# Attention and a two-layer MLP on one core: two loads of q and k issued in front of two copies on GpSimd

## The chip, the core and the metric

The kernel runs on one core of a Trainium2 chip. The core has a matrix engine (TensorE, PE in the profile), a vector engine (VectorE, DVE), an activation engine (ScalarE, ACT), a general-purpose engine (GpSimd, POOL) and a queue engine (SyncE, SP) that here only issues transfers. Transfers between the chip's memory (HBM) and on-chip memory, and transposes done in flight, run on 16 DMA engines that all queues share. The metric is the device time of one execution in microseconds (us). Before the change it was 387.28 us, the median of three runs (386.26 to 387.37).

## The reference

Attention with 12 heads for 8 sequences of 448 tokens, then a two-layer MLP with a leaky ReLU over the 3584 tokens that come out:

```python
scores = (1 / sqrt(64)) * q @ k.T             # q, k, v: 8 x 12 x 448 x 64, float32
attn   = exp(scores - scores.max()) / sum      # softmax over the keys
x      = (attn @ v), heads side by side        # 3584 x 768
h      = x @ w_in                              # 768 x 2048
out    = maximum(0.01 * h, h) @ w_out          # 2048 x 768, float32 out
```

## The kernel before

**Units and chunks.** Attention is cut into 48 *units* u: one batch and one pair of heads each. A unit goes through these steps. Its q, k and v are loaded from HBM and cast to bf16 on the way (`load_soft`, L143, a DMA issued from GpSimd's queue for two units at a time; the names in the profile are fq, fk, fv). GpSimd copies q and k into an interleaved tile qkb (`cast`, L172) and v into a tile with a column of ones (L174). qkb is transposed into qkT: for units 0 to 14 on TensorE (`transposes`, L268, with a VectorE copy, L274), from unit 15 on by a DMA transpose from SyncE's queue (`dma_transposes`, which calls `turn`, L251). Each unit has four *chunks* of 112 keys. `scores` (L285) multiplies two heads of a chunk on TensorE, `expo` (L294) takes the exponential on ScalarE, and `rows` (L802, L808, L809) multiplies by v, divides by the sum and gives x. x is transposed into xT, mostly by DMA transposes of SyncE too (L251).

**The MLP.** The 3584 tokens are cut into seven blocks (`cuts`). For each, products with w_in (L366 and L662 in the first block, L483 in the others) give h, and products with w_out (L620, L555) give the output; most are done by a scheme with seven products in place of eight, for which VectorE forms sums and differences of weights and of x. MLP products are always on TensorE between the pieces of attention, so that ScalarE's exponentials run beside them.

**Order.** Every engine works its own queue in the order in which the program issues instructions; the program writes that order out by hand. After units 0 to 5, scores come in *bursts* of three chunks: burst g holds the chunks 3g to 3g+2, so burst 20 begins unit 15 and burst 21 ends it and begins unit 16. Between bursts, `place` interleaves MLP products and rows by a small model of the times. With each burst of the first block `place` calls `feed(g)`, which fills the queues of GpSimd and SyncE for units to come:

```python
def feed(g):
    t, r = divmod(g, 4)
    u = 3 * t
    if r < 3:
        if g >= 16: ahead = u + 6 + r
        for x, y in enumerate(("q", "cast")):
            cast(u + 3 + r, (x,))      # copy q, then k, of one unit
            fetch(1)
    ...
    pay()                              # copies of v that are due
    if r < 3:
        ahead = max(ahead, u + 5 + r)
        fetch()                        # loads up to unit `ahead`
```

`fetch` issues the next pair loads of q, k and v, as long as their first unit is not beyond `ahead` and the copies are close enough behind (unit u is loaded only once unit u-3 has been copied). So `feed(13)` copies q and k of unit 13, `feed(14)` those of unit 14. At g = 13 the lines give t = 3, r = 1, u = 9 and `ahead` = 15; at g = 14, `ahead` = 16, so the loads of q and k of units 16 and 17 are issued in `feed(14)`, behind unit 14's copies.

**Buffers.** Loads go to two buffers each for fq, fk and fv, so units 16/17 take those that units 12/13 had. qkb has three buffers, qkT four. Each load increments one of eight semaphores in turn. The w_out matrix arrives in four loads (L185) issued on GpSimd's queue just before.

Of the kernel before, what the change touches and what calls it, by code (L numbers as in the profile page):

```python
# [16 lines left out]
def kernel(  # L17
# [146 lines left out]
    def cast(u, parts=(0, 1, 2), by=nc.gpsimd.tensor_copy):  # L164
        if u >= NU:
            return
        for x in parts:
            f = raw[u].pop(x)
            if x < 2 and u not in qk_sb:
                qk_sb[u] = cast_pool.tile([SC, 2, NSC, 2, D], BF16, name="qkb")  # L170
            if x < 2:
                by(qk_sb[u][:, x].rearrange("p so h d -> p h so d"), f)  # L172
            else:
                by(v_sb[u % NV][:, :, :, :D], f)  # L174
# [6 lines left out]
    def load_w(n=1):  # L181
        for _ in range(n):
            if w_steps:
                o, i = w_steps.pop(0)
                nc.gpsimd.dma_start(out=o, in_=i)  # L185
# [67 lines left out]
    def dma_transposes(u):  # L253
        if NPE <= u < NU:
            turn(qkT[u % NQ][:, :QL], qk_sb[u].rearrange("p i so h d -> p (i so h d)"))
# [589 lines left out]
    ahead = 0  # L845

    def fetch(n=3):
        for x, y in enumerate(("q", "cast", "v")):
            u = to["load"][x]
            if n and u <= ahead and u - 3 < to[y]:  # L850
                load_soft(u, 2, (x,))
                to["load"][x] += 2
                n -= 1

    def pay():
        while owed_v and owed_v[0] < rows_done + NV:
            cast(owed_v[0], (2,))
            to["v"] = owed_v.pop(0) + 1
        fetch()

    def feed(g):
        nonlocal ahead
# [3 lines that stand above are left out]
            if g >= 16:  # L866
                ahead = u + 6 + r
            for x, y in enumerate(("q", "cast")):
                cast(u + 3 + r, (x,))
                to[y] = u + 4 + r  # L870
                fetch(1)
            owed_v.append(u + 3 + r)
        pay()
        if r < 3:
            ahead = max(ahead, u + 5 + r)
            fetch()
            load_w({9: 1, 10: 3}.get(g, 0))
        if r > 0:
            dma_transposes(u + 2 + r)
            to["turn"] = max(to["turn"], u + 3 + r)  # L880
# [4 lines left out]
    def place(i, want, soon=0, full=True, calm=True, first=False, lazy=0, keen=NU, cap=NU):  # L885
# [3 lines left out]
        while True:  # L889
# [21 lines left out]
            if want > done and state < 2 and turned(last) and not blocked and len(slots) == 3 and all(  # L911
                x <= now + 0.05 + 0.2 * j for j, x in enumerate(at)
            ):
                state = 2
                order = list(slots)
                start = chunk
                burst(lazy)
                if first:
                    feed(start // 3)
                done += 1  # L920
                for x, t in enumerate(order[:chunk - start]):
                    model["act"] = max(model["act"], now + 0.45 + 0.2 * x) + 0.8
                    free[id(t)] = model["act"] + (0.3, 0.15 + 0.5 * (lazy > 1), 0.15 + 0.5 * lazy)[x]
                    if (start + x) % NSC == NSC - 1:
                        ready[(start + x) // NSC] = model["act"] + 0.1
                model["now"] = now + 0.78
                continue
# [115 lines left out]
```

## Time and profile before

| | us |
|---|---|
| median of the runs (three) | 387.28 |
| lowest, highest | 386.26, 387.37 |
| the profiled execution, whole | 386.85 |
| its span on the core | 385.1 |
| in its span: TensorE busy | 374.7 |
| ScalarE busy | 264.3 |
| VectorE busy | 232.8 |
| GpSimd busy | 141.9 |

The span reaches from the first to the last instruction of the profiled execution, whose own time is 1.75 us longer. The granted TensorE clock is 1.0 throughout. In the rows that follow, a timeline line gives the start in us, the length in us, the engine, the line of the kernel, the operation, output and inputs, the count, and in brackets the idle time ahead of it and what ended that. SPq and POOLq are the queues of DMA issues. A line of windows gives the stretch, its length, the busy time of PE, PE's weight loads, DVE, ACT and POOL, each with a count of instructions, then the granted clock, the DMA engines' mean share and the GB/s they moved. The share of the DMA engines can be over 1, since transfers of several queues overlap. A line of DMA issues ends with the size and the us from issue to landing.

### The profile page before, as it was taken

The numbers are of one execution on the slowest core, as the hardware profiler recorded it, in microseconds if no ns is written. First come the engines' busy times: TensorE is split into PE (matmuls) and PEld (weight loads), VectorE is DVE, ScalarE is ACT, GpSimd is POOL, SyncE is SP. The second block draws the span as 40 slices with busy tenths as digits, with TensorE's granted clock in tenths as the row PEclk, the third lists the DMA queues.
The fourth block names the chain that finished last, engine by engine and source line by source line (L and its number), as shares of the span: only waits on it lengthen the run. The fifth ranks groups of instructions, "written<-read, shape, count | busy, mean of one in ns | idle before, by whom it ended". The sixth has DMA issues, their size and how long they took to land.

```text
span 385.1 us, 10021 instructions
## 1 busy us (share of the span) xinstructions
PE 374.7 (97%) x4095; PEld 259.4 (67%) x4095; DVE 232.8 (60%) x488; ACT 264.3 (69%) x391; POOL 141.9 (37%) x223
## 2 busy tenths in 40 slices
PE   7999999979999999999999999999999999999995
PEld 3665558745588655886558865678656895668753
DVE  3662946835867646657469574576745665474753
ACT  6997886745767877687765877767776687717700
POOL 6988750765455443620436304353042100000000
PEclk9999999999999999999999999999999999999999
DMA  8999999799979958991499913899229600330022
GB/s 165 183 195 203 183 189 203 90 138 205 165 126 129 140 91 161 199 131 26 74 183 171 146 26 56 179 184 156 27 48 182 140 15 3 107 81 26 3 82 83
DMA packets 93278, 47.09 MB, mean 122 GB/s; under 512 B 51888, under 2 KB 89904, under 8 KB 93232
## 3 DMA queue, kind: packets, MB, share of 16 engines
q0 software_dynamic: 37536, 22.24, 45.7%
q1 hardware_dynamic: 55056, 23.66, 32.1%
q8 instruction: 32, 0.52, 0.6%
q10 hardware_dynamic: 640, 0.56, 0.5%
q14 instruction: 14, 0.11, 0.1%
HBM read 45.61 MB, written 11.01 MB: 147 GB/s over the span
## 4 chain that ended last, share of the span: by engine, by line
PE 76%; DMA 16%; POOL 5%; issue 2%; ACT 0%; DVE 0%; POOLq 0%; ACTq 0%
PE g L555 31%; PE g L483 14%; PE sc L483 14%; PE sc L802 8%; PE sc L285 7%; DMA fk<-in_k_dram 5%; DMA fq<-in_q_dram 4%; DMA w_mix<-in_v_dram 3%; POOL qkb L172 2%; DMA qkT<-qkb 2%; DMA w_in_mix<-in_v_dram 1%; POOL v L174 1%; PE g L620 1%; DMA hmix<-in_q_dram 1%; POOL fk L143 1%
## 5 line engine op out<-in xcount | busy, mean ns | idle before, releaser
L294 ACT ACTIVATE e<-sc 112x896 bf16<-112x896 f32 x192 | 162.7, 920 | 49.2 <-PE sc L285 49.2
L555 PEld LDWEIGHTS <-h 128*128 128x128 bf16 x632 | 57.2, 98 | 44.2 <-issue 12.4
L555 PE MATMUL g<-w_out_sb,h 128*128 128x384 bf16 x416 | 81.0, 326 | 0.0
L472 ACT ACTIVATE h<-c 128x512 bf16<-128x512 f32 (+1 forms) x72 | 43.5, 611 | 25.5 <-DVE c L498 17.2
L483 PEld LDWEIGHTS <-w_in_sb 128*128 128x128 bf16 x576 | 54.3, 98 | 6.0
L285 PE MATMUL sc<-qkT 64*128 64x448 bf16 x384 | 50.2, 353 | 4.7 <-DMA qkT<-qkb 3.0
L172 POOL COPY qkb<-fq 112x512 bf16<-112x512 bf16 x38 | 26.2, 689 | 73.5 <-DMA fq<-in_q_dram 41.4
L174 POOL COPY v<-fv 112x512 bf16<-112x512 bf16 x38 | 25.0, 667 | 69.9 <-PE sc L802 69.8
L802 PEld LDWEIGHTS <-e 112*128 112x128 bf16 x1344 | 46.2, 97 | 4.5 <-ACT e L294 0.2
L802 PE MATMUL sc<-v,e 112*128 112x65 bf16 x1344 | 47.7, 193 | 0.0
L483 PEld LDWEIGHTS <-w_in_mix 128*128 128x128 bf16 x432 | 41.2, 98 | 4.1
L560 DVE COPY o<-g 128x384 f32<-128x384 f32 x49 | 27.2, 554 | 22.3 <-PE g L555 22.2
L555 PE MATMUL g<-w_mix,h 128*128 128x384 bf16 (+1 forms) x208 | 38.3, 323 | 0.0
L285 PEld LDWEIGHTS <-qkT 64*128 64x128 bf16 x384 | 15.7, 94 | 32.2 <-issue 19.5
L563 DVE TENSOR_TENSOR o<-o,g 128x384 f32<-128x384 f32 x39 | 21.6, 553 | 18.0 <-PE g L555 15.9
L809 DVE TENSOR_TENSOR x<-sc,rec 112x512 bf16<-112x512 f32 x42 | 29.0, 692 | 1.5
L808 DVE RECIPROCAL rec<-sc 112x8 f32<-112x8 f32 x42 | 8.7, 207 | 34.8 <-PE sc L802 31.4
L172 POOL COPY qkb<-fk 112x512 bf16<-112x512 bf16 x38 | 24.5, 645 | 13.4 <-DMA fk<-in_k_dram 13.3
L483 PE MATMUL g<-xT,w_in_sb 128*128 128x256 bf16 (+1 forms) x216 | 28.5, 268 | 0.0
L483 PE MATMUL sc<-xT,w_in_sb 128*128 128x256 bf16 (+1 forms) x216 | 28.5, 268 | 0.0
L555 PE MATMUL g<-w_mix,hmix 128*128 128x384 bf16 x104 | 20.1, 326 | 0.0
L483 PE MATMUL g<-x_mix,w_in_mix 128*128 128x256 bf16 (+1 forms) x144 | 19.0, 268 | 0.0
(106 smaller groups left out, 475.4 us busy)
## 6 DMA issues: line engine op xcount, KB each, us to landing
fq<-in_q_dram POOLq DMA_DIRECT2D x19, 224.0 KB, 6.5
fk<-in_k_dram POOLq DMA_DIRECT2D x19, 224.0 KB, 7.5
fv<-in_v_dram POOLq DMA_DIRECT2D x19, 224.0 KB, 5.8
w_in_sb<-in_moe_w_in_dram POOLq DMA_DIRECT2D x4, 768.0 KB, 11.6
w_out_sb<-in_moe_w_out_dram POOLq DMA_DIRECT2D x4, 768.0 KB, 18.4
out_dram<-o SPq DMA_DIRECT2D x7, 336.0 KB, 4.5
out_dram<-o SPq DMA_DIRECT2D x8, 288.0 KB, 3.7
out_dram<-o SPq DMA_DIRECT2D x7, 240.0 KB, 3.8
```

The lines of the kernel that those rows point to most:

```text
L172: by(qk_sb[u][:, x].rearrange("p so h d -> p h so d"), f)
L174: by(v_sb[u % NV][:, :, :, :D], f)
L285: nc.tensor.matmul(ps[:, j, :S], t[j * D:(j + 1) * D, S + c * SC:S + c * SC + P], t[j * D:(j + 1) * D, :S], start=True, stop=True,)
L294: nc.scalar.activation(e[:, :, c, :], sc_t.pop((u, c))[:SC, :, :S], AX.Exp, scale=scale)
L472: nc.scalar.activation(hs[:, m:m + 2, cols], x.rearrange("p (m t) -> p m t", m=2), AX.Prelu, alpha=0.01)
L483: nc.tensor.matmul(ps[:, j * nh:(j + 1) * nh], w[:, kk, ts(j, P)], x[:, kk], start=(first and j == 0 and kk == 0), stop=(kk == KH - 1), sk ...
L555: nc.tensor.matmul(ps[:, cols], x[:, m], w[:, m], start=(first and m == 0), stop=(m == MH - 1), skip_group_check=True,)
L560: by(o[:, at], ps[:, :NW])
L563: nc.vector.tensor_add(o[:, at], o[:, at], ps[:, :NW])
L802: nc.tensor.matmul(ps[:, j, qc, :D + 1], e[:, at:at + P], vt[:, j, c, :D + 1], start=(c == 0), stop=(c == NSC - 1),)
L808: nc.vector.reciprocal(rec, ps[:SC, :, :, D:D + 1])
L809: nc.vector.tensor_mul(x_t[u].rearrange("p q j d -> p j q d"), ps[:SC, :, :, :D], rec.to_broadcast([SC, 2, NSC, D]))
```

## The change

One line of `feed` is changed:

```diff
         pay()
         if r < 3:
-            ahead = max(ahead, u + 5 + r)
+            ahead = max(ahead, u + (6 if g >= 13 else 5) + r)
             fetch()
             load_w({9: 1, 10: 3}.get(g, 0))
```

For g = 13 `ahead` becomes 16 instead of 15, so `feed(13)` issues the loads of q and k of units 16 and 17 at its end. For g = 14 it becomes 17 instead of 16, which allows no load that was not allowed before, and from g = 16 on the earlier line in `feed` gives the same value as before. GpSimd's queue is the only one whose order is changed:

```diff
 L172 copy qkb<-fq   (unit 13)
 L172 copy qkb<-fk   (unit 13)
-L172 copy qkb<-fq   (unit 14)
-L172 copy qkb<-fk   (unit 14)
 L143 load fq        (units 16, 17)
 L143 load fk        (units 16, 17)
+L172 copy qkb<-fq   (unit 14)
+L172 copy qkb<-fk   (unit 14)
 L174 copy v<-fv     (unit 13)
 L143 load fv        (units 16, 17)
```

All instructions, their sizes and their number are the same, and so are the orders of TensorE, VectorE, ScalarE and SyncE.

## The prediction

> **What bounds the kernel now.** I read the busy shares first, then TensorE's list of waits, the chain of waits that ended last, and the timelines of the queues that this chain names.
>
> ```profile
> span 385.1 us, 10021 instructions
> PE 374.7 (97%) x4095; PEld 259.4 (67%) x4095; DVE 232.8 (60%) x488; ACT 264.3 (69%) x391; POOL 141.9 (37%) x223
> ...
> PE   7999999979999999999999999999999999999995
> ...
> PE sc L285 <- DMA qkT<-qkb: 3.0, 2, 2.6
> ```
>
> TensorE (PE) is busy for 374.7 of 385.1 us, so only a gap on PE can be won. In the forty slices it is below 9 tenths in the first, the last and the ninth (77 to 87 us). The last row heads PE's list of waits (total us, times, longest) and is its only one for a DMA: 3.0 us in two waits of the scores (L285) for transposed q and k (qkT), which is the ninth slice's gap. PE's timeline places the two waits:
>
> ```profile
> 83.64 0.74 PE L285 MATMUL sc<-qkT 64*128 64x448 bf16 x6 [2.60 <-DMA qkT<-qkb]
> ...
> 86.37 0.36 PE L285 MATMUL sc<-qkT 64*128 64x448 bf16 x2
> 87.13 0.55 PE L285 MATMUL sc<-qkT 64*128 64x448 bf16 x4 [0.40 <-DMA qkT<-qkb]
> ```
>
> Bursts of three chunks and four chunks to a unit make the six products at 83.64 the first of unit 15 (burst 20, chunks 60 to 62). Burst 21 begins with unit 15's last chunk at 86.37 and goes on to unit 16 at 87.13. Without waits they would have started at 81.04 (83.64 - 2.60) and 84.13 (87.13 - 0.40 - 2.60). From unit 15 on the transposes are DMAs of SyncE (SP), so the next question is what made those late. Two pieces of the chain of waits (start, us, what), then the timelines of SP and GpSimd (POOL) answer it:
>
> ```profile
> 32.12 15.31 DMA fq<-in_q_dram
> ...
> 80.11 6.97 DMA qkT<-qkb
> ```
>
> ```profile
> 76.33 1.22 SPq L251 DMA_TRANSPOSE qkT<-qkb  x1
> ```
>
> ```profile
> 52.88 0.62 POOL L172 COPY qkb<-fk 112x512 bf16<-112x512 bf16 x1
> 68.02 0.81 POOL L172 COPY qkb<-fq 112x512 bf16<-112x512 bf16 x1 [14.52 <-DMA fq<-in_q_dram]
> 69.00 0.71 POOL L172 COPY qkb<-fk 112x512 bf16<-112x512 bf16 x1 [0.17 <-DMA fk<-in_k_dram]
> 69.66 0.70 POOL L143 DMA_DIRECT2D fq<-in_q_dram  x1
> 70.35 0.70 POOL L143 DMA_DIRECT2D fk<-in_k_dram  x1
> 71.05 0.62 POOL L174 COPY v<-fv 112x512 bf16<-112x512 bf16 x1
> 72.71 0.71 POOL L143 DMA_DIRECT2D fv<-in_v_dram  x1 [1.04 <-issue]
> ...
> 74.98 0.70 POOL L143 DMA_DIRECT2D fq<-in_q_dram  x1 [0.31 <-POOL qkb L172]
> 75.68 0.62 POOL L172 COPY qkb<-fk 112x512 bf16<-112x512 bf16 x1
> ...
> 79.46 0.62 POOL L172 COPY qkb<-fk 112x512 bf16<-112x512 bf16 x1
> ```
>
> POOL ends unit 13's copies at 53.50 (52.88 + 0.62), sits idle for 14.52 us until unit 14's loads land, and is then a queue without a gap it could close by itself: copies of 14, loads of 16/17, v, copies of 15 (ending at 76.30, when SP issues transpose 15 at 76.33), loads of 18/19, copies of 16 (ending at 80.08; transpose 16 at 80.11). So the two waits of PE hang on POOL's work after 68.02 and on how long each transpose takes in flight.
>
> **The change, part by part.** Two load issues, q and k of units 16/17, leave their place behind unit 14's copies (69.66 and 70.35) for the place behind unit 13's copies (53.50). Nothing is added or removed; the loads cross only unit 14's two copies in POOL's queue, and no other queue changes its order.
>
> (1) *POOL's time after 68.02.* What followed the two issues started at 71.05 and can now start at 69.66: 1.39 us earlier. The copies of 15 and 16 wait for no transfer there, so transpose 15 is issued at 74.94 (76.33 - 1.39) and 16 at 78.72 (80.11 - 1.39). The row at 72.71 shows 1.04 us of idle where a load behind a copy elsewhere waits 0.31 (the row at 74.98); if this extra 0.73 went away too, the shift would be 2.12. I take 1.39, as no row says what the extra belongs to.
>
> (2) *The new place.* The 1.40 us of issuing (2 x 0.70) lies in the 14.52 us in which POOL waited. The buffers are those of units 12/13, free once unit 13's copies end, so the q load waits some 0.3 us; the k load also waits for the first w_out piece, which had the same semaphore:
>
> ```profile
> L185 POOL DMA_DIRECT2D w_out_sb<-in_moe_w_out_dram x1: 752/752/752, 39.8 to 39.8; - x1
> ...
> DMA to landing us min/median/max: 14.4/14.4/14.4
> ```
>
> It landed at 54.2 (39.8 + 14.4), before the k load's turn (53.50 + 0.30 + 0.70 = 54.50). Cost nothing, covered by 12.8 us (68.02 - 55.2). Without that cover each microsecond would delay unit 14's copies by as much, and PE's own transposes of 14, at 71.76, would be next:
>
> ```profile
> 71.76 0.56 PE L268 MATMUL sc<-c,qkb 112*128 112x112 bf16 x8
> ```
>
> (3) *The DMA engines.* Here are the windows from 66 to 78 us (the last two columns are the DMA share and GB/s), then the landings of the loads issued at 49.67, 50.37 and 51.07:
>
> ```profile
> 66.00:68.00 2.00, 1.97 (x22) 1.33 (x21) 1.23 (x3) 1.95 (x4) 0.00 (x0) 1.00 1.22 164
> 68.00:70.00 2.00, 2.00 (x31) 2.00 (x29) 1.97 (x3) 1.53 (x3) 1.81 (x3) 1.00 0.20 27
> 70.00:72.00 2.00, 2.00 (x48) 2.00 (x45) 1.90 (x4) 1.53 (x4) 1.68 (x3) 1.00 0.46 50
> 72.00:74.00 2.00, 2.00 (x20) 0.95 (x18) 1.54 (x3) 1.08 (x2) 1.29 (x3) 1.00 1.25 160
> 74.00:76.00 2.00, 2.00 (x15) 1.05 (x15) 1.30 (x4) 1.90 (x3) 1.69 (x4) 1.00 1.12 130
> 76.00:78.00 2.00, 2.00 (x25) 1.23 (x23) 0.85 (x3) 1.91 (x3) 1.62 (x3) 1.00 0.88 94
> ...
> fq<-in_q_dram POOLq DMA_DIRECT2D x1, 224.0 KB, 18.2
> fk<-in_k_dram POOLq DMA_DIRECT2D x1, 224.0 KB, 18.6
> fv<-in_v_dram POOLq DMA_DIRECT2D x1, 224.0 KB, 19.0
> ```
>
> They landed at 67.9, 69.0 and 70.1, in the order of issue and 1.1 us apart: POOL's transfers pass through in order, so two more behind them delay none of them. Behind them the engines almost emptied (shares 0.20 and 0.46); there the moved transfers fit and should land at 71.2 and 72.3 at the same spacing. Now they are issued at 69.66 and 70.35 and stand at the head of what follows, as the landings of q16 and k16 and then of v16 (issued at 72.71), k18 and the two transposes show:
>
> ```profile
> fq<-in_q_dram POOLq DMA_DIRECT2D x1, 224.0 KB, 4.0
> fk<-in_k_dram POOLq DMA_DIRECT2D x1, 224.0 KB, 4.9
> ...
> fv<-in_v_dram POOLq DMA_DIRECT2D x1, 224.0 KB, 4.7
> ...
> fk<-in_k_dram POOLq DMA_DIRECT2D x1, 224.0 KB, 7.1
> qkT<-qkb SPq DMA_TRANSPOSE x1, 7.3
> qkT<-qkb SPq DMA_TRANSPOSE x1, 7.0
> qkT<-qkb SPq DMA_TRANSPOSE x1, 3.0
> ```
>
> q16 landed at 73.7, k16 at 75.3, v16 at 77.4, k18 at 83.7 and transpose 15 at 83.6 (76.33 + 7.3): each load entered before the one ahead of it had landed. With q16 and k16 gone, v16 is issued at 71.32 (72.71 - 1.39) into an empty queue and takes between 4.0 us (q16, alone) and 4.7, landing at 75.3 to 76.0, which is 1.4 to 2.1 us earlier; what queues behind should keep its spacing to v16. So transpose 15's flight shrinks by 0 to 0.7 us beyond the shift. The last row, transpose 17 issued at 84.8, bounds the flight from below: 3.0 us.
>
> The arbitration between the two kinds of transfer is the open size. The Trainium skill, "DMA: Bandwidth & Descriptors", section "Queues, rings and completion order", says that a DMA engine takes turns between the queues that have work, packet by packet. By that rule a transpose gets its turns however long the other queue is, so shortening the backlog without emptying it would leave the 7.3 us as they are and the gain would be the bare shift. The rows fit it in part: flights of 7.3 and 7.0 us beside loads, 3.0 us where the backlog was nearly through.
>
> (4) *The sum.* Lower bound, shift alone: transpose 15 lands at 82.24 (wait 1.20 instead of 2.60), transpose 16 at 85.69 (78.72 + 6.97) against a need at 84.13 + 1.20 = 85.33; unit 16's scores start about 1.4 us earlier. Upper bound: transpose 15 in time for 81.04 (flight 6.1 or less) and 16 for 84.13 (5.4 or less): all 3.0. Both lie within the flights seen, 3.0 to 7.3. I take 1.9: the shift of 1.39 and 0.5 of the possible 0.7, since v16 would meet a queue as empty as q16's. After 90 us PE waits for no DMA, and loads, copies and transposes of later units hang on the same queues and move with it, so PE keeps the gain. The profiled execution took 386.85 us (385.1 and 1.75 around the span): 384.95 after. The runs' median is 387.28, 0.43 above it, so the forecast for the median is 387.28 - 1.9 = 385.4.
>
> **The rivals.** *A. The bare shift.* The flights keep 7.3 and 6.97: 387.28 - 1.4 = 385.9. The turn-taking rule of the Trainium skill, cited above, would bring this about. For it: a share of 0.88 or more in the windows from 72 to 78, where v16, q18 and k18 stay beside transpose 15. Against it: the 3.0 us flight.
>
> *B. The gap at 72.71 is tied to the clock and not to the copy ahead of it.* Then POOL's v16 load, and all behind it, stays where it is; the shift is lost, and only the emptier DMA queue is left: v16 lands at 76.7 instead of 77.4, worth at most 0.7 us: 386.6, not to be told from no change. For it: 1.04 us "issue" for which the profile names no releaser. Against it: nothing that landed then is known.
>
> *C. Slower: POOL is held at one of the two moved issues.* Here a load is held until transfers ahead of it have landed, because too much is outstanding. POOL runs in order, so unit 14's copies are held with it. Held until v of 14/15 lands at 70.1, POOL starts unit 14's q copy at 70.8 (0.70 for the issue), ends both at about 72.2, against 71.05 for the same point now: transpose 15 is 1.15 us later, and PE's own transposes of 14 wait 0.4 us at 71.76. PE then loses about 1.2: 388.5, and more with a longer hold. It decides once the second issue ends after 69.4 (68.02 + 1.39). Against it: near 44 us four w_out pieces of 768 KB and the loads of units 10/11 (the first of them, in the chain above, from 32.12 to 47.4) were outstanding, and the last three w_out issues show no hold:
>
> ```profile
> 42.19 2.23 POOL L185 DMA_DIRECT2D w_out_sb<-in_moe_w_out_dram x3
> ```
>
> At 54.5 it would be three w_out pieces and five loads of 224 KB: 3424 KB (3 x 768 + 5 x 224) against 3744 (4 x 768 + 3 x 224) then.
>
> *D. Everything.* Both waits go: 387.28 - 3.0 = 384.3. It needs transpose 15 in 6.1 us.
>
> **How the numbers follow.** About 0.3% (1.16 us) is what a measurement of this kernel can tell from no change. Chances: forecast (gain 1.6 to 2.6) 0.32, A 0.18, D 0.14, B or another loss of the shift 0.21, C or another loss 0.15. Faster by over 0.3% are the forecast, A and D, 0.64, less 0.02 for runs of A that fall short of 1.16: 0.62. Within 0.3%: B and those, 0.23. Slower: 0.15. The likeliest case's own range is 384.3 to 385.9, from D to A. For eight in ten it goes to 384.0 (D with the 0.3 of scatter) and up to 387.5 (B whole, with scatter), which leaves out C.
>
> **What would show it.** Right: two load issues on POOL between 53.5 and 55.3; unit 14's copies still at 68.0; the v copy behind them at about 69.7; DMA shares from 68 to 72 near those before 68, and emptier from 72 to 74; transpose 15 issued near 74.9; PE's wait for qkT under 1.6 us in all, with no new wait elsewhere. A shows as flights of 7 us, B as a v16 load still at 72.7, C as copies of unit 14 after 68.5. I am wrong altogether if unit 14's loads land later than 68, or if PE's gain near 87 us is given back to another wait before the end.

## The result and the profile after

The changed kernel took 385.94 us (median of 20 executions, 383.84 to 386.96) against 386.90 us for the kernel before in the same comparison (20 executions, 386.13 to 390.18). The ratio is 0.9959 with a 95% interval of 0.9942 to 0.9976, so it is faster by 0.9 to 2.2 us, 1.6 us at the centre. (The means, 387.25 and 385.67 us, lie 1.58 us apart, the medians 0.96.) Two more comparisons gave 0.9987 (0.9962 to 1.0011) and 0.9957 (0.9936 to 0.9978). The profiled execution took 386.51 us, 384.7 of them in the span; that is 0.34 us less than the profiled execution of before, where the prediction had 1.9.

The page of the changed kernel (busy time, then PE's row of the forty slices), and below it PE's list of waits:

```profile
span 384.7 us, 10021 instructions
PE 375.0 (97%) x4095; PEld 259.5 (67%) x4095; DVE 232.7 (60%) x488; ACT 263.9 (69%) x391; POOL 140.8 (37%) x223
...
PE   7999999989999999999999999999999999999995
```

```profile
PE sc L285 <- DMA qkT<-qkb: 2.0, 2, 1.1
PE g L216 <- DVE c L211: 1.2, 1, 1.2
PE sc L285 <- ACT e L294: 0.8, 3, 0.4
PE g L268 <- ACT qkb L239: 0.6, 1, 0.6
```

The ninth slice rose from 7 to 8, and the two waits for qkT fell from 3.0 to 2.0 us. The last row is a wait in the first microseconds that the profiled execution of before did not have; with it and what else differs in the start, PE reached burst 18 at 73.54 instead of 72.90. PE's timeline has both waits at the same two places as before:

```profile
73.54 0.74 PE L285 MATMUL sc<-qkT 64*128 64x448 bf16 x6
...
82.82 0.74 PE L285 MATMUL sc<-qkT 64*128 64x448 bf16 x6 [1.15 <-DMA qkT<-qkb]
...
86.82 0.55 PE L285 MATMUL sc<-qkT 64*128 64x448 bf16 x4 [0.90 <-DMA qkT<-qkb]
```

GpSimd's timeline shows the moved loads and what followed from them:

```profile
54.06 0.71 POOL L143 DMA_DIRECT2D fq<-in_q_dram  x1
55.11 0.70 POOL L143 DMA_DIRECT2D fk<-in_k_dram  x1 [0.33 <-issue]
68.37 0.69 POOL L172 COPY qkb<-fq 112x512 bf16<-112x512 bf16 x1 [12.56 <-DMA fq<-in_q_dram]
69.47 0.61 POOL L172 COPY qkb<-fk 112x512 bf16<-112x512 bf16 x1 [0.42 <-DMA fk<-in_k_dram]
70.03 0.94 POOL L174 COPY v<-fv 112x512 bf16<-112x512 bf16 x1
72.01 0.71 POOL L143 DMA_DIRECT2D fv<-in_v_dram  x1 [1.04 <-issue]
...
74.89 0.75 POOL L172 COPY qkb<-fk 112x512 bf16<-112x512 bf16 x1
```

Both loads are issued while GpSimd would have waited anyway. The copy of v follows unit 14's first copy by 1.66 us (70.03 - 68.37); before it was 3.03 (71.05 - 68.02), so 1.37 us are gained there. The copy of v then takes 0.94 us where it took 0.62, and the gap of 1.04 us ahead of the next load is still there. At the load of v 1.05 us are left of the shift (72.01 - 68.37 = 3.64, before 72.71 - 68.02 = 4.69). In SyncE's timeline 1.01 us are left at unit 15's transpose (75.67 - 68.37 = 7.30, before 76.33 - 68.02 = 8.31):

```profile
75.67 1.23 SPq L251 DMA_TRANSPOSE qkT<-qkb  x1
```

The windows of the changed kernel from 68 to 76 us (the last two columns are the DMA share and GB/s):

```profile
68.00:70.00 2.00, 2.00 (x25) 1.63 (x22) 1.94 (x3) 1.53 (x3) 1.21 (x2) 1.00 1.46 197
70.00:72.00 2.00, 2.00 (x48) 2.00 (x46) 1.97 (x5) 2.00 (x4) 0.97 (x2) 1.00 0.89 121
72.00:74.00 2.00, 2.00 (x25) 1.30 (x23) 1.63 (x3) 0.61 (x2) 1.87 (x3) 1.00 0.25 27
74.00:76.00 2.00, 2.00 (x15) 1.09 (x12) 1.11 (x4) 2.00 (x3) 1.51 (x3) 1.00 0.88 107
```

The hole in the transfers has moved: at 68 to 70 us the share is 1.46 instead of 0.20, and the engines are nearly idle from 72 to 74, where they had a share of 1.25. The landing rows of v of 16/17, q of 18/19 and the transposes of units 15 and 16 show who profits:

```profile
fv<-in_v_dram POOLq DMA_DIRECT2D x1, 224.0 KB, 3.6
...
fq<-in_q_dram POOLq DMA_DIRECT2D x1, 224.0 KB, 4.1
...
qkT<-qkb SPq DMA_TRANSPOSE x1, 7.1
...
qkT<-qkb SPq DMA_TRANSPOSE x1, 7.3
```

The loads that come next land sooner (3.6 instead of 4.7 us, 4.1 instead of 5.0). The transposes, for which TensorE waits, fly as long as before (7.3 and 7.0).

### The profile page after: what moved, and what is told of

Same layout as the page of the kernel before. It is cut to its first block, busy times and chain, and to the rows that moved or that the text cites. A ratio compares the mean times of both kernels' runs of the same rounds, so it can differ in the third digit from the quotient of the medians.

```text
span 384.7 us, 10021 instructions
## 1 busy us (share of the span) xinstructions
PE 375.0 (97%) x4095; PEld 259.5 (67%) x4095; DVE 232.7 (60%) x488; ACT 263.9 (69%) x391; POOL 140.8 (37%) x223
## 4 chain that ended last, share of the span: by engine, by line
PE 91%; ACT 3%; DMA 3%; DVE 1%; issue 1%; POOL 1%; DVEq 0%; ACTq 0%; POOLq 0%
PE g L555 31%; PE g L483 14%; PE sc L483 14%; PE sc L285 11%; PE sc L802 10%; PE g L366 4%; ACT e L294 3%; PE g L662 2%; DMA qkT<-qkb 2%; PE g L620 2%; DMA hmix<-in_k_dram 1%; PE g L268 1%; PE g L304 1%; PE sc L366 1%; PE g L331 0%
```

## The experiments

Two theories stood against each other. By *shift*, TensorE gains what GpSimd's queue gains, and no more. By *relief*, it gains because two transfers are gone from the head of the DMA queue. All ratios are to the kernel before, run on the same chip.

**The shift taken back, the early loads kept** (e1_pad):

```diff
             owed_v.append(u + 3 + r)
+            if g == 14:
+                for f in pad:                  # unit 14's raw q and k
+                    nc.gpsimd.tensor_copy(f, f)
         pay()
```

> The changed kernel with two idle copies on GpSimd (unit 14's q and k raw tiles copied onto themselves) right where the moved loads used to be, about 1.4 us of GpSimd time. The early loads stay early. Theory 'shift' (the gain is GpSimd's 1.39 us alone): the gain is gone, ratio to before 0.999 to 1.001, TensorE's two waits for qkT back at about 3.0 us, transpose flights 7 us. Rival 'relief' (the gain comes from two transfers less at the head of the DMA queue): at least half of the gain stays, ratio 0.996 to 0.998, flights of the transposes of units 15 and 16 shorter than 6.5 us.

Ratio 1.0015 (0.9998 to 1.0031): the gain is gone. GpSimd's timeline shows the two idle copies and unit 15's k copy:

```profile
69.75 0.94 POOL L878 COPY fq<-fq 112x512 bf16<-112x512 bf16 x1
70.63 0.94 POOL L878 COPY fk<-fk 112x512 bf16<-112x512 bf16 x1
...
76.13 0.62 POOL L175 COPY qkb<-fk 112x512 bf16<-112x512 bf16 x1
```

They took 1.8 us, somewhat more than the 1.4 planned. By the times, relief is out, as it asked for 0.996 to 0.998. The one profile does not show where the gain went. Its flights were 6.6 and 6.1 us, the second shorter than relief asked for, and its two waits for qkT came to 2.0 us, as in the changed kernel, with TensorE at burst 18 (73.52, changed kernel 73.54) and at burst 22 (90.92 and 90.99) at almost the same times. The 1.6 us by which its span is longer (386.3 against 384.7) come later, most of them in two waits for VectorE that neither the profile of before nor that of the changed kernel has:

```profile
PE sc L288 <- DMA qkT<-qkb: 2.0, 2, 1.7
...
PE g L486 <- DVE x_mix L433: 0.8, 1, 0.8
PE g L558 <- DVE o L566: 0.6, 1, 0.6
```

A wait like the last one also stands in a profile without the idle copies (0.8 us in e10 below), so whether the copies cause these waits stays open. That the gain hangs on the shift rests here on the twelve times and not on this profile.

**Half of the change** (e3_q_only): the load of q in front of unit 14's copies, the load of k between them.

```diff
-            fetch()
+            fetch(1 if g == 13 else 3)
```

> Half of the change: only the load of q of units 16/17 goes in front of unit 14's copies; that of k is issued between unit 14's two copies. 'Shift': 0.70 us of GpSimd time is gained, TensorE's waits for qkT about 2.3 us against 3.0 before, ratio 0.998 (half of the change). 'Relief' would also give about half. A threshold (gain only once both are moved) would give 1.000.

Ratio 0.9987 (0.9965 to 1.0010), where 0.998 was expected; the interval holds no change as well. The waits came to 0.9 us, with TensorE late (burst 18 at 74.25). It tells little.

**The shift the other way.** The same idle copies in the kernel before, two (e6_before_pad) and one (e9_before_pad_half):

```diff
             owed_v.append(u + 3 + r)
+            if g == 14:
+                for f in pad:                  # one copy: pad[:1]
+                    nc.gpsimd.tensor_copy(f, f)
         pay()
```

> The kernel before with two idle copies on GpSimd (about 1.4 us) behind unit 14's copies: the shift the other way. 'Shift': TensorE's waits for qkT grow by about 1.4 us to 4.4 us, ratio 1.003 to 1.004. If the lateness of GpSimd there does not set the time (a threshold, or slack between it and TensorE): ratio 0.999 to 1.001.

> The kernel before with one idle copy on GpSimd behind unit 14's copies, about 0.9 us, half of the pad that cost 4.1 us (ratio 1.0107). 'Clock' (a wait of TensorE of 4 to 5 us lets the granted clock drop to 0.5 for some 3 to 4 us, and shorter ones do so now and then): the time grows by more than 0.9 us, ratio 1.004 to 1.007, with single executions 1.5 to 2 us apart; where the profile shows a wait over 4 us in one piece, the clock is below 1.0 in the windows behind it. 'One for one': ratio 1.002 to 1.003 and a clock of 1.0 throughout.

Two copies (0.93 us each, 1.8 together and not the 1.4 planned) gave a ratio of 1.0107 (1.0066 to 1.0149), 4.1 us. PE's timeline and the windows behind the wait (the third column from the end is the granted clock) show where they went:

```profile
87.98 1.11 PE L288 MATMUL sc<-qkT 64*128 64x448 bf16 x6 [5.07 <-DMA qkT<-qkb]
```

```profile
88.00:89.00 1.00, 1.00 (x6) 0.20 (x6) 0.00 (x0) 0.55 (x1) 1.00 (x2) 0.61 1.35 241
89.00:90.00 1.00, 1.00 (x6) 0.48 (x5) 0.00 (x0) 1.00 (x2) 1.00 (x3) 0.50 0.35 75
90.00:91.00 1.00, 1.00 (x5) 0.50 (x4) 0.00 (x0) 0.98 (x2) 1.00 (x3) 0.50 0.60 116
91.00:92.00 1.00, 1.00 (x6) 0.53 (x5) 0.00 (x0) 0.00 (x0) 1.00 (x2) 0.68 0.92 117
```

The wait is 2.1 us longer than the 3.0 of before, and behind it TensorE's clock is down for four windows, which costs another 1.7 us of work (0.39 + 0.50 + 0.50 + 0.32). Unit 15's transpose also flew 8.8 us here, where it flew 7.3 before. The six executions tell the clock's share apart: five had a granted clock of 0.990 to 0.996 and took 390.95 to 392.40 us, and the one that kept 1.000 took 388.81, which is 1.95 us above the median of before (386.86) and close to the 1.8 us of the copies.

One copy gave 1.0020 (0.9997 to 1.0042), one for one and short of what the clock theory expected, in an interval that holds no change as well. Its profiled execution had waits of 1.13 and 0.50 us and a clock of 1.00; its two longest executions, 389.29 and 390.11 us, had 0.994 and 0.996, the other ten 0.998 or more.

**Fewer loads beside the transposes.** In the changed kernel, the loads of units 18/19 are issued later. A flag holds them in `fetch`: q and k alone until unit 16's copies (e2_qk18_late), all three until unit 16's (e4_all18_late) or unit 17's copies (e7_all18_later, g == 18).

```diff
-            if n and u <= ahead and u - 3 < to[y]:
+            if n and u <= ahead and u - 3 < to[y] and not (held and x < 2):   # all three: not held
...
+        if g == 16:
+            held = True
...
+        if g == 17:                            # behind unit 16's copies
+            held = False
+            fetch()
         pay()
```

> The changed kernel with the loads of q and k of units 18 and 19 moved behind unit 16's copies. If the 7 us flights come from loads in flight beside the transposes: unit 15's transpose is issued 0.7 us or more earlier than in the changed kernel and flies under 5 us, both waits of TensorE for qkT fall to 0.3 us or less, ratio to before 0.991 to 0.993. If the flights come from something else (the transposes themselves, the transpose of x between them): flights stay at 6.5 to 7.5 us, and the gain over the changed kernel is GpSimd's shift alone, about 1.0 us at unit 15 and 1.5 to 2 us at unit 16; ratio 0.992 to 0.994, so the flights tell the two apart. A third outcome: unit 18's copies become late and TensorE waits at burst 24.

> As e2_qk18_late, and the load of v of units 18/19 goes behind unit 16's copies as well, so that unit 15's transpose meets no load that is issued after it until unit 16's copies end. If loads beside the transposes set the flights: unit 15's transpose flies 3 to 4.5 us, unit 16's still meets the three loads; both waits gone, ratio 0.991 to 0.993. If not: flights of 6.5 us or more.

> The changed kernel with all loads of units 18/19 behind unit 17's copies, so that neither unit 15's nor unit 16's transpose has a load issued beside it. If loads beside a transpose set its flight: both fly 3 to 4.5 us (against 7.1 and 7.3 in the changed kernel, 3.5 and 8.8 where only unit 16's met the loads). If the order of the transposes or their own traffic sets it: unit 16's still takes 6 us or more. The time is open: the copies of units 18 to 21 come several us later and may make TensorE wait at burst 24 or later.

The landing rows of the transposes of units 15 and 16 in e7, where unit 15's has no load issued beside it and unit 16's one only in its last microsecond:

```profile
qkT<-qkb SPq DMA_TRANSPOSE x1, 3.3
...
qkT<-qkb SPq DMA_TRANSPOSE x1, 2.9
```

So the loads set the flights: about 3 us without them, about 7 beside them. In e4 the flights were 5.2 and 6.9 us, no wait for qkT was left, and the ratio was 0.9956 (0.9941 to 0.9972). e7 itself took 389.74 us in its one execution, since the held loads, and with them the copies of units 18 to 20, became late and TensorE waited 2.9 us at burst 26:

```profile
107.31 0.36 PE L285 MATMUL sc<-qkT 64*128 64x448 bf16 x2 [2.92 <-DMA qkT<-qkb]
```

In e2 unit 15's transpose flew 3.5 us and unit 16's, issued amid three loads, 8.8. The profiled execution was at 384.73 us with one wait of 0.3 us, yet the times spread from 384.0 to 391.2 us and the ratio, without the longest, was 1.0018 (0.9989 to 1.0048). Because of that spread the kernel was profiled twice more.

> The kernel with q and k loads of 18/19 behind unit 16's copies, once more, because its times fell in two groups (384.0 to 385.2 and 387.9 to 389.6) and the profile came from the faster one. If the slower group comes from the wait for unit 16's transpose (8.8 us beside three loads): an execution near 389 us shows a wait for qkT of over 2 us or a clock below 1.0 behind one. If it comes from elsewhere: no such wait, and the time is lost at another place.

> The same kernel a third time, for a look at the other group of times: same expectations as for the second.

They took 388.25 and 386.90 us. PE's timeline and the landing of unit 16's transpose in the first of them:

```profile
87.95 0.55 PE L285 MATMUL sc<-qkT 64*128 64x448 bf16 x4 [3.13 <-DMA qkT<-qkb]
```

```profile
qkT<-qkb SPq DMA_TRANSPOSE x1, 10.8
```

In the other the flight was 10.2 us and the wait 1.9. One transpose beside the same three loads thus landed after 8.8, 10.2 or 10.8 us, and the time went with it. The clock was 1.00 in both. In the first comparison the four slowest executions, 389.11 to 391.18 us, had a granted clock of 0.994 to 0.996, the other eight, up to 389.00 us, 0.998 or more. So the slowest lost clock as well; behind which wait, no profile shows.

**The two candidates again** (e5_change_again, e12_change_third: the change; e8_e4_again: all loads of 18/19 behind unit 16's copies):

> The changed kernel itself once more, so that it stands beside the others on one chip. Ratio to before 0.994 to 0.998 as in its first runs. TensorE's waits for qkT between 0.5 and 2 us, depending on how late TensorE reaches burst 20 in the profiled execution; flights of the transposes of units 15 and 16 again 6.5 to 7.5 us.

> The kernel with all loads of units 18/19 behind unit 16's copies, once more. If it removes the wait for good: ratio to before 0.993 to 0.997 and below that of the changed kernel by 0.1 to 0.4%, no wait for qkT in the profile. If its first result was the luck of a chip: not below the changed kernel.

> The changed kernel a third time, since its first two comparisons gave ratios of 0.9959 and 0.9987 whose intervals overlap between 0.9962 and 0.9976. If GpSimd's net shift of about 1.0 us at the load of v is what TensorE gains: ratio 0.996 to 0.998, waits of TensorE for qkT of 1 to 2 us. The full gain of the forecast (1.9 us) would be 0.995.

The change gave 0.9987 and 0.9957, the other kernel 0.9958 (0.9926 to 0.9989), at a median of 385.11 us against 386.25 for the change on the same chip. Its profile has no wait for qkT, with a flight of 3.1 us for unit 15's transpose, although three loads were issued behind it from 1.6 us on, as in e4, where the same transpose took 5.2:

```profile
PE g L216 <- DVE c L211: 1.2, 1, 1.2
PE g L268 <- ACT qkb L239: 0.9, 1, 0.9
PE sc L285 <- ACT e L294: 0.8, 3, 0.4
PE sc L285 <- DVE qkT L274: 0.2, 1, 0.2
```

It was steady at 0.9956 and 0.9958, but the change's three ratios overlap with these, so that it is the better kernel is likely and not shown.

## Why the prediction was right, and which of its terms was not

**What bounds the kernel.** Right. TensorE's only wait for a DMA stands at bursts 20 and 21, and the time moves with GpSimd's queue: with the shift taken back the gain was gone (1.0015), and the opposite shift cost time (1.0107). Half of each, 0.9987 and 1.0020, points the same way within the noise. TensorE also kept what it had won, as predicted: burst 22 began 0.31 us earlier (90.99 against 91.30), and the span was 0.4 us shorter.

**Part (1), 1.39 us of shift.** Its size held at the place named (1.37 us, up to the copy of v) and 0.32 us were lost one step further: that copy, moved forward, ran beside VectorE's differences of two weight tiles and took 0.94 us instead of 0.62. VectorE's timelines of the changed kernel, then of the kernel before:

```profile
70.42 1.43 DVE L383 TENSOR_TENSOR w_mix<-w_out_sb,w_mix 128x768 bf16<-128x768 bf16 x2
```

```profile
69.16 1.84 DVE L383 TENSOR_TENSOR w_mix<-w_out_sb,w_mix 128x768 bf16<-128x768 bf16 x2
71.03 0.21 DVE L808 RECIPROCAL rec<-sc 112x8 f32<-112x8 f32 x1
```

Before, the copy started at 71.05, as the last of these ended; now it starts at 70.03, among them. The Trainium skill ("SBUF — State Buffer", section "Who interferes with whom") says that a VectorE instruction with two inputs in SBUF contends with a GpSimd instruction that reads SBUF; the rows agree, with 0.94 us beside such an instruction and 0.62 behind it. The prediction priced the moved work by its old length and did not look at what it would then stand beside. In e3 the loss fell on the other side: GpSimd's copies at 69.88 and 70.44 took 0.62 us each, and the two differences of L383 beside them 2.37 us together, against 1.43 in the row at 70.42. No run moved VectorE's work, so that it is the cause is read off the timelines.

**Part (2), the new place costs nothing.** Right: GpSimd still waited 12.56 us for unit 14's loads, and the k load waited only 0.33 us. Rival C, a hold at the moved issues, did not occur.

**Part (3), the flights.** This is the term that was mis-sized: the 0.5 us by which a shorter queue was to shorten the flights measured nothing beyond the scatter (7.1 and 7.3 us against 7.3 and 7.0; in the repeats 7.4 and 7.3, 6.9 and 6.5; in e1, with the same loads moved, 6.6 and 6.1). The load of v did land 1.8 us earlier (75.6 against 77.4), as forecast, but the transpose behind it did not keep its distance to it. The prediction took the length of the queue ahead of a transpose for what delays it. The runs show that it is the loads beside it. In e2 and its two repeats, in e7 and in e8 a transpose flew 2.9 to 3.5 us with at most one earlier load still in flight and the next issued 0.8 us or more behind it. It flew 6.5 to 7.4 us in the changed kernel, where the loads of units 18/19 are in flight or issued beside it, and 8.8 to 10.8 us where a load of q was issued just ahead of it and one of k just behind. The rule is not sharp, as the 5.2 us in e4 and the 8.8 us in e6 show. The unchanged flights are rival A. The turn-taking rule of the Trainium skill ("DMA: Bandwidth & Descriptors", section "Queues, rings and completion order"), which the prediction weighed and set aside, agrees with the 7.1 and 7.3 us; the 8.8 to 10.8 us it does not give by itself.

**Rival B.** The gap of 1.04 us was tied to its place in the queue and not to the clock: it ended at 72.71 before and at 72.01 now, and it had the same length in every run. What it is stays open.

**The signs.** Two of those that the prediction named went against it. TensorE's two waits came to 2.0 us and not under 1.6. And unit 14's loads landed after 68, with the first copy at 68.37, which was to mean that the prediction is wrong altogether. It does not mean that here, as the whole execution was late by then: unit 13's copies ended at 54.14 (53.51 + 0.63) instead of 53.50, and in the repeats unit 14's first copy stands at 67.77 and 67.65.

**The sum.** Forecast 1.9 us, measured 1.6 (0.9 to 2.2), with 0.5 and 1.7 in the repeats. The two misses, 0.3 us of shift and 0.5 us of flight, leave 1.1 (1.9 - 0.3 - 0.5). Unit 14's chain shows somewhat less: from its first copy to unit 16's scores it took 19.1 us before (87.13 - 68.02), and 18.5 (86.82 - 68.37), 18.8 and 17.7 us in the three profiles of the change, 0.8 less on average. But it took 18.8 us in e1 too (86.75 - 68.00), so single profiles do not tell the two kernels apart. The rest up to 1.6 is not accounted for, so that the measured centre came within 0.3 us of the forecast is in part luck. The forecast of 385.4 us also started from 387.28, the median of three runs, where twenty gave 386.90; the measured median of 385.94 is rival A's time. One profiled execution of before is a thin base, and two things that the sum did not hold vary between executions: when TensorE reaches burst 18 (72.90 to 74.87 us in the profiles), and whether a wait is long enough for the clock to fall.

## What to carry to other kernels

An issue that stands behind a wait in an in-order queue delays everything behind it by its own time; moved ahead of the wait it is free, as long as its buffers and semaphores are. The gain is then what the queue gains: look at what the work behind it will stand beside, for a copy moved by 1.4 us lost 0.3 to a neighbour. And if a transpose in flight is the last link, look at the loads issued beside it before those ahead of it: issued behind it, they left it a flight of about 3 us instead of 7 (5.2 once, in e4), though holding them one unit too long made the next units late (e7).

## What the hardware showed that was not expected

A wait of TensorE of 5.07 us lowered its granted clock to 0.50 for about four microseconds behind it (e6), and two idle copies of 1.8 us cost 4.1. Waits of 2.60, 2.92 and 3.13 us left the clock at 1.00. The Trainium skill ("TensorE: Matmul & The Clock Gate", section "What's actually happening") says that the gate falls to half rate after an idle window of about 3.4 us and that the window is free-running; the four waits agree with it. So the stall of 5.07 us was worth more than its own time; from which length on that is so, between 3.13 and 5.07 us, no run shows.
